# A decode block on one core: attention on two kv heads at a time with 32 KB descriptors and V as the moving operand, projections in row form

## The chip, the cores and the metric

One core of a Trainium2 chip runs the whole program. The metric is the device time of one execution in microseconds (us), as the median of the fast runs. PE is TensorE, DVE VectorE, ACT ScalarE, POOL GpSimd, SP SyncE, whose queue issues the loads. The kernel before takes 445.8 us.

## The reference, cut to what matters

One decode step of a block with adaptive layer norm, batch 8, all in bf16:

```python
mod = silu(c) @ w_mod                            # 8 x 6144: sa, ca, ga, sb, cb, gb
h = layernorm(x) * (1 + ca) + sa
q = h @ wq                                       # 32 heads of 128
o = softmax(q @ k_cache.T * 128**-0.5) @ v_cache # 8 x 4 kv heads, 8192 keys each, 8 q heads per kv head
x = x + ga * (o @ wo)
h = layernorm(x) * (1 + cb) + sb
x = x + gb * ((relu(h @ W_gate) * (h @ W_up)) @ W_down)
```

K and V are 134 MB, all weights 51 MB; every byte is used once. There are 32 pairs of batch and kv head ("heads" below); each has 2 MB of K and 2 MB of V.

## The kernel before

All large loads go through one ring in SBUF, `arena`, of nine 16 KB slots per partition. `load` only notes a transfer; `pump` is called after every operation and issues the next transfers, in order, on SP, as soon as the program has an operation that reads what lies in their place. The transfer itself then waits (by semaphore) until those reads are done. So the order of the loads is fixed, and a load that waits for its place holds back all the loads behind it.

```python
SLOT = 8192; NSLOT = 9                           # elements of bf16: 16 KB per partition
def pump():
    while stream:
        key, src, n = stream[0]
        lo = cursor[0] if cursor[0] + n <= NSLOT * SLOT else 0
        if P.unread("arena", lo, lo + n):
            return
        ...
        P.op("sp", lambda e: e.dma_start(dst, src), writes=[slot_r(lo, lo + n)], dma=True)
...
for n in range(N):                               # 32 heads: K, then V, 128 rows of 16 KB each
    load(("k", n), A_k_cache[n // G, n % G].rearrange("(p c) d -> p (c d)", p=128), SLOT)
    load(("v", n), A_v_cache[n // G, n % G].rearrange("(p c) d -> p (c d)", p=128), SLOT)
for i in range(4):
    load(("wo", i), wo_src[i], SLOT)             # "(q h d) n -> q d h n": rows of 2 KB
...
```

The attention turns K on DVE in quarters (`kt_part`), multiplies it with a padded q (`qk_part`, 512 columns moving), takes the maximum (`rowmax`, `spread`, `headmax`), the exponential on ACT (`expo`), turns it on DVE (`p_turn`), and multiplies with V (`pv`). In `pv`, V is the stationary operand, 64 weight loads of 128 x 128 for each head, and only 8 columns move:

```python
for cc in range(NC):                             # 64
    fns.append(lambda e, cc=cc: e.matmul(ps[:, 3, col:col + J], vv[:, cc, :], pv_[:, cc % 16, cc // 16, :], ...))
...
for n in range(N):
    kt_part(n + 1, 0)
    if n >= 1: p_turn(n - 1)
    kt_part(n + 1, 1)
    qk_part(n, 0); qk_part(n, 1); qk_part(n, 2); qk_part(n, 3)
    kt_part(n + 1, 2)
    if n >= 1: pv(n - 1)
    rowmax(n)
    kt_part(n + 1, 3)
    spread(n); headmax(n); expo(n); make_qpad(n + 2)
```

Gate and up are formed with weights stationary and 8 columns moving, too (448 matmuls); the output and down projections already stream weight rows of 256 columns through four column tiles of 32.

## Time and profile before

| | before |
|---|---|
| time, median | 445.8 us |
| span in the profile | 444.1 us |
| bytes moved, mean rate | 186 MB, 419 GB/s |
| DMA in the chain of waits | 83% |
| last weight landed (first engine / last engine) | 434.4 / 440.3 us |

From the profile's page of the kernel before: the span; the rows of forty slices (PEclk is the granted clock in tenths); the DMA queues; the chain; groups of instructions (count, busy us, mean ns, idle before them); two rows of DMA issues, with the us from issue to landing.

```profile
span 444.1 us, 7822 instructions
PE 290.9 (66%) x3514; PEld 165.4 (37%) x3514; DVE 217.7 (49%) x333; ACT 33.2 (7%) x78; POOL 30.8 (7%) x141
...
DMA  8999999999999999999999999999999999999993
GB/s 344 421 428 425 434 434 428 426 429 437 427 428 432 431 426 426 435 434 425 426 434 429 425 429 435 429 425 432 429 430 428 429 421 403 422 430 429 426 429 151
...
q8 instruction: 27, 0.44, 0.4%
...
DMA 83%; PE 8%; DVE 7%; issue 1%; ACT 0%; SPq 0%; POOL 0%; DVEq 0%; ACTq 0%; POOLq 0%
...
L411 DVE STREAM_TRANSPOSE kt<-arena 128x1024 uint32<-128x1024 uint32 x128 | 153.3, 1218 | 114.6 <-DMA arena<-in_A_k_cache_dram 114.6
L420 PE MATMUL ps<-kt,qpad 128*128 128x512 bf16 x512 | 161.5, 482 | 2.0 <-POOL qpad L400 2.0
...
L460 PE MATMUL ps<-pT,arena 128*128 128x8 bf16 x2048 | 56.0, 166 | 49.2 <-DVE pT L450 49.2
...
arena<-in_A_k_cache_dram SPq DMA_DIRECT2D x32, 2048.0 KB, 25.7
arena<-in_A_v_cache_dram SPq DMA_DIRECT2D x32, 2048.0 KB, 30.2
```

The GB/s row is flat near 430 from the second slice to the last but one; the one dip, 403, is the output weights. K is issued 25.7 us and V 30.2 us before it lands: with 4.9 us for a load of 2 MB, five to six loads are queued at any time.

Stretches of the attention of the kernel before (columns: stretch, its length, busy us of PE, of its weight loads, DVE, ACT and POOL with instruction counts, then the granted clock, the DMA share and GB/s):

```profile
180.00:240.00 60.00, 44.47 (x495) 24.18 (x496) 38.03 (x56) 4.67 (x12) 4.87 (x24) 0.80 1.01 430
240.00:300.00 60.00, 46.06 (x499) 23.84 (x498) 37.80 (x58) 4.67 (x12) 4.87 (x24) 0.81 1.01 430
300.00:360.00 60.00, 43.26 (x493) 23.38 (x492) 37.02 (x56) 5.44 (x14) 4.05 (x20) 0.82 1.01 429
```

The trace also records each DMA packet. Most packets of one size last the same time; these are medians of the kernels before and after, in ns:

```
bytes of a packet   2,048  4,096  8,192  14,336  16,384  24,576  28,672  32,768
took                   84    159    309     535     611     912   1,062   1,213
```

A packet starts 4 ns before the one ahead of it ends. The slope, (912 - 611) ns for 8,192 bytes, is 27.2 B/ns for an engine, and about 5 ns are left for each packet whatever its size.

### The profile page before, as it was taken

Reading aid. Unit: us, or ns where it says so; the run is one execution under the profiler, and the core shown is the slowest. Engines: PE = TensorE matmul, PEld = TensorE weight load, DVE = VectorE, ACT = ScalarE, POOL = GpSimd, SP = SyncE. Lnnn points to the kernel's source line nnn. Section 1 sums busy time; section 2 is a strip of 40 time slices with the busy share of each in tenths; the row PEclk is TensorE's granted clock in tenths of the full one; section 3 lists DMA queues with packets and bytes.
Section 4 is the critical chain, followed back from the end, with each engine's and each line's share of the span. In section 5 each row is a group of like instructions: output and inputs, shape, how many; then the busy total and the mean of one; then the engine's idle time right before and its main releaser. Section 6 shows DMA issues by size and latency. Waiting matters only on the chain.

```text
span 444.1 us, 7822 instructions
## 1 busy us (share of the span) xinstructions
PE 290.9 (66%) x3514; PEld 165.4 (37%) x3514; DVE 217.7 (49%) x333; ACT 33.2 (7%) x78; POOL 30.8 (7%) x141
## 2 busy tenths in 40 slices
PE   0235355677858676776877767786777787558753
PEld 0111022344434333443433334343333345348741
DVE  0503065666655566666555566665556664230000
ACT  0200010000001000000100000001000002000000
POOL 4000020100000001000000110000001000000000
PEclk9995576887788888879688888778888869655555
DMA  8999999999999999999999999999999999999993
GB/s 344 421 428 425 434 434 428 426 429 437 427 428 432 431 426 426 435 434 425 426 434 429 425 429 435 429 425 432 429 430 428 429 421 403 422 430 429 426 429 151
DMA packets 16770, 186.14 MB, mean 419 GB/s; under 512 B 1537, under 2 KB 1633, under 8 KB 5985
## 3 DMA queue, kind: packets, MB, share of 16 engines
q1 hardware_dynamic: 16704, 185.64, 98.5%
q8 instruction: 27, 0.44, 0.4%
q14 instruction: 7, 0.05, 0.0%
q10 hardware_dynamic: 32, 0.01, 0.0%
HBM read 185.63 MB, written 0.02 MB: 418 GB/s over the span
## 4 chain that ended last, share of the span: by engine, by line
DMA 83%; PE 8%; DVE 7%; issue 1%; ACT 0%; SPq 0%; POOL 0%; DVEq 0%; ACTq 0%; POOLq 0%
DMA arena<-in_A_k_cache_dram 62%; DMA arena<-in_B_W_down_dram 8%; DMA arena<-in_A_wq_dram 7%; DMA arena<-in_A_wo_dram 4%; PE ps L460 4%; DVE kt L411 3%; DMA c_r<-in_c_dram 2%; PE ps L528 1%; DVE pT L450 1%; PE ps L334 1%; PE ps L420 1%; PE ps L357 0%; DVE lu L281 0%; ACT L278 0%; DVE hT L286 0%
## 5 line engine op out<-in xcount | busy, mean ns | idle before, releaser
L411 DVE STREAM_TRANSPOSE kt<-arena 128x1024 uint32<-128x1024 uint32 x128 | 153.3, 1218 | 114.6 <-DMA arena<-in_A_k_cache_dram 114.6
L420 PE MATMUL ps<-kt,qpad 128*128 128x512 bf16 x512 | 161.5, 482 | 2.0 <-POOL qpad L400 2.0
L420 PEld LDWEIGHTS ps<-kt,qpad 128*128 128x128 bf16 x512 | 60.9, 119 | 91.8 <-issue 60.6
L460 PE MATMUL ps<-pT,arena 128*128 128x8 bf16 x2048 | 56.0, 166 | 49.2 <-DVE pT L450 49.2
L460 PEld LDWEIGHTS ps<-pT,arena 128*128 128x128 bf16 x2048 | 54.1, 96 | 63.6 <-issue 63.3
L400 POOL COPY qpad<-qR 32x32 bf16<-32x32 bf16 x128 | 26.0, 203 | 312.8 <-PE ps L420 256.0
L430 PE MATMUL ps<-identf,negm 128*128 128x128 f32 x64 | 20.2, 408 | 37.0 <-DVE negm L426 37.0
L444 ACT ACTIVATE prb<-ps,bias 128x512 bf16<-128x512 f32 x32 | 22.0, 687 | 283.9 <-DVE mjt L438 283.9
L528 PE MATMUL ps<-hT,arena 128*128 128x8 bf16 x448 | 24.8, 194 | 7.7 <-DMA arena<-in_B_W_up_dram 3.0
L528 PEld LDWEIGHTS ps<-hT,arena 128*128 128x128 bf16 x448 | 24.4, 153 | 8.1 <-DMA arena<-in_B_W_up_dram 3.2
L430 PEld LDWEIGHTS ps<-identf,negm 128*128 128x128 f32 x64 | 12.3, 240 | 40.3 <-DVE negm L426 40.3
L450 DVE STREAM_TRANSPOSE pT<-prb 128x512 bf16<-128x512 bf16 x32 | 21.5, 672 | 1.7 <-ACT prb L444 1.7
L426 DVE TENSOR_REDUCE negm<-ps 128x1 f32<-128x512 f32 x32 | 20.9, 653 | 1.0 <-PE ps L420 1.0
L535 DVE TENSOR_TENSOR hmT<-ps,grel 128x224 bf16<-128x224 f32 x1 | 0.4, 391 | 30.7 <-ACT grel L533 30.7
L357 PE MATMUL ps<-arena,hT 128*32 128x512 bf16 x64 | 7.6, 627 | 11.2 <-DMA arena<-in_A_wq_dram 8.4
L303 PE MATMUL ps<-st,sel 128*128 128x1 f32 x4 | 1.2, 362 | 19.3 <-DVE st L302 19.3
L334 PE MATMUL ps<-arena,hT 128*32 128x512 bf16 x96 | 9.0, 544 | 6.8 <-DMA arena<-in_w_mod_dram 6.8
L545 PE MATMUL ps<-arena,hmT 128*32 128x256 bf16 x112 | 7.1, 415 | 7.4 <-DMA arena<-in_B_W_down_dram 7.4
L509 PE MATMUL ps<-arena,oT 128*32 128x256 bf16 x128 | 6.4, 382 | 5.2 <-DMA arena<-in_A_wo_dram 2.6
L341 DVE COPY mod<-ps 128x512 f32<-128x512 f32 x2 | 1.3, 670 | 15.2 <-PE ps L334 15.2
L436 DVE TENSOR_REDUCE mj<-ps 128x8 f32<-128x128 f32 x32 | 8.1, 252 | 1.2 <-PE ps L430 1.2
L303 PEld LDWEIGHTS ps<-st,sel 128*128 128x128 f32 x4 | 1.0, 310 | 19.6 <-DVE st L302 19.6
(64 smaller groups left out, 66.0 us busy)
## 6 DMA issues: line engine op xcount, KB each, us to landing
arena<-in_A_k_cache_dram SPq DMA_DIRECT2D x32, 2048.0 KB, 25.7
arena<-in_A_v_cache_dram SPq DMA_DIRECT2D x32, 2048.0 KB, 30.2
arena<-in_w_mod_dram SPq DMA_DIRECT2D x4, 3072.0 KB, 18.2
arena<-in_A_wq_dram SPq DMA_DIRECT2D x4, 2048.0 KB, 35.0
arena<-in_A_wo_dram SPq DMA_DIRECT2D x4, 2048.0 KB, 19.1
arena<-in_B_W_gate_dram SPq DMA_DIRECT2D x4, 1792.0 KB, 24.2
arena<-in_B_W_up_dram SPq DMA_DIRECT2D x4, 1792.0 KB, 28.0
arena<-in_B_W_down_dram SPq DMA_DIRECT2D x3, 1792.0 KB, 33.8
```

The source lines that it names most:

```text
L334: fns.append(lambda e, w=w, pr=pr, j=j, kk=kk: e.matmul(ps[32 * j:32 * j + 32, pr, :], hT[:, kk, :], w[:, 2 * pr:2 * pr + 2, j, :], start= ...
L357: fns.append(lambda e, w=w, z=z, g=g, kk=kk: e.matmul(ps[32 * g:32 * g + 32, 3 + z, :], hT[:, kk, :], w[:, g, z, :], start=(kk == 0), stop ...
L400: P.op("pool", lambda e, n=n, Q=Q: e.tensor_copy(qpad[32 * Q:32 * Q + 32, n % NQ, :, 24 + 32 * Q:32 + 32 * Q], qR[32 * Q:32 * Q + 32, :, n ...
L411: P.op("dve", lambda e: e.transpose(ktb[:, to:to + QE].bitcast(dt.uint32), arena[:, lo:lo + QE].bitcast(dt.uint32)), reads=[slot_r(lo, lo ...
L420: fns.append(lambda e, t=t, r=r: e.matmul(ps[:, n % 2, :].rearrange("p (c k) -> p c k", k=32), qpad[:, n % NQ, t * 2 + r, 24 - 8 * i:152 - ...
L426: P.op("dve", lambda e: e.tensor_reduce(negm[:, n % 2:n % 2 + 1], ps[:, n % 2, :], AX.X, ALU.max, negate=True), reads=[bank(n % 2)], write ...
L430: P.op("pe", lambda e: e.matmul(ps[:, 2, 0:128], negm[:, n % 2:n % 2 + 1].to_broadcast([128, 128]), identf[:], start=True, stop=True), rea ...
L436: P.op("dve", lambda e: e.tensor_reduce(mj[:, z, :], ps[:, 2, 0:128].rearrange("p (m j) -> p j m", j=J), AX.X, ALU.min), reads=[bank(2)], ...
L444: P.op("act", lambda e: e.activation(prb[:, z, :], ps[:, z, :], ACT.Exp, bias=bias[:, z:z + 1], scale=scale, accum_out=lall[:, n:n + 1]), ...
L450: P.op("dve", lambda e: e.transpose(pT[:, z, :], prb[:, z, :]), reads=[R("prb", z, z + 1)], writes=[R("pT", z, z + 1)])
L460: fns.append(lambda e, cc=cc: e.matmul(ps[:, 3, col:col + J], vv[:, cc, :], pv_[:, cc % 16, cc // 16, :], start=(cc == 0), stop=(cc == NC ...
L528: fns.append(lambda e, w=w, f=f, kk=kk, off=off, first=first: e.matmul(ps[:, 0, off + f * B:off + (f + 1) * B], w[:, f // FR, f % FR, :], ...
```

## The change

The intent is fewer, longer DMA descriptors and fewer PE instructions: K and V come for two heads at once, 128 rows of 32 KB; V becomes the moving operand (512 columns) against the turned probabilities on two column tiles of 64; output, gate, up and down all stream weight rows, loaded in rows of up to 32 KB.

```diff
-        wo_src = A_wo.rearrange("(q h d) n -> q d h n", q=4, d=128)
+        wo_src = A_wo.rearrange("(p k) n -> p (k n)", k=KO)
...
-        for n in range(N):
-            load(("k", n), A_k_cache[n // G, n % G].rearrange("(p c) d -> p (c d)", p=128), SLOT)
-            load(("v", n), A_v_cache[n // G, n % G].rearrange("(p c) d -> p (c d)", p=128), SLOT)
-        for i in range(4):
-            load(("wo", i), wo_src[i], SLOT)
+        for m in range(M):                       # M = 16 pairs of heads
+            for nm, t in (("k", A_k_cache), ("v", A_v_cache)):
+                load((nm, m), t[m // 2, 2 * (m % 2):2 * (m % 2) + 2].rearrange("g (p c) d -> (g p) (c d)", p=64), 2 * SLOT)
+        wo_parts = [(0, 16), (16, 32)]
+        gu_parts = [(0, 4), (4, 8)]
+        wd_parts = [(0, 14), (14, 21), (21, 25), (25, 27), (27, 28)]
...
-        ktb = sb("kt", [128, 2 * SLOT], dt.bfloat16)
+        ktb = sb("kt", [128, 6 * 2048], dt.bfloat16)
...
+        def pv(m):                               # 32 matmuls of 512 columns for a pair
+            vv = arena[:, lo:lo + 2 * SLOT].rearrange("p (h i c d) -> p h c i d", h=2, i=4, d=Dh)
+            for t in range(32):
+                fns.append(lambda e, t=t: e.matmul(
+                    ps[64 * (t % 2):64 * (t % 2) + 64, 5, :].rearrange("p (i d) -> p i d", d=Dh),
+                    pT[:, z, t].rearrange("p g x -> p (g x)"), vv[:, t // 16, t % 16], ...,
+                    tile_position=(0, 64 * (t % 2))))
+        def fold(m):                             # four masked reads of PSUM on DVE, then one small matmul
...
+        for m in range(M):
+            for e8 in range(8):
+                kt_part(m, e8)
+                qk_part(m, e8)
+                if m >= 1:
+                    if e8 == 0:
+                        rowmax(m - 1, 1); spread(m - 1)
+                    elif e8 == 1:
+                        headmax(m - 1); expo(m - 1)
+                    elif e8 == 3:
+                        p_turn(m - 1)
+                    elif e8 == 4:
+                        pv(m - 1)
+                    elif e8 == 7:
+                        fold(m - 1)
+                if e8 == 5:
+                    rowmax(m, 0)
+            make_qpad(m + 2)
```

The ring is still nine slots of 16 KB, so four pair loads of 32 KB fit (K, V, K, V) and 16 KB are never used in the attention. The load of V for pair m+2 takes the place of V of pair m.

## The prediction

> **What bounds the kernel now.** HBM reading. The chain of waits is 83% DMA; the slices show the DMA engines full at 421 to 437 GB/s from the second slice on, except 403 where the output weights load. In the attention stage (60 to 360 us, table of stretches) PE is 0.7 to 0.75 busy, DVE 0.62. The Trainium skill ("DMA: Bandwidth & Descriptors", Specifications) puts the fabric ceiling at 435 GB/s. The trace agrees: its packet records last 611 ns for 16 KB, 912 for 24 KB, 84 for 2 KB: 27.2 B/ns per engine (435 GB/s on 16), plus about 5 ns per packet (a packet overlaps the next by 4 ns). So bandwidth can gain only about 1%.
>
> **What the change saves, per DMA engine (estimates from these durations).** KV: 512 packets of 607 ns become 256 of about 1,209: 1.3 us. Output weights: 256 of 80 ns become 16 of 1,209: 1.1 us. Gate, up: 0.1 us. 39 fewer DMAs, 6 ns for each semaphore packet: 0.2 us. Instruction fetches: 27 packets of 16 KB, which fit the 7,028 PE instructions, cost about 605 ns each, apparently on eight engines in turn (3.4 each). Moving V turns 2,048 PV matmuls into 512, and row form 448 gate/up matmuls into 128, so PE instructions halve and the engines that finish last gain about 1 us. All is on the critical path, because the DMA never pauses: 3.5 us together. The tail (bandwidth falls off from 434 to 440 us as engines finish apart, then 4 us of matmuls, two DVE ops, store) stays.
>
> **What it adds.** Per pair of heads (19.4 us of DMA) DVE rises from 13.6 us to about 16: two 64-partition turns of 1,024 columns (1.2 us each) and a fold of four PSUM reads (1.1 us), less one head-max. PE: QK as before (228 ns a matmul at full clock, 427 at half); PV as 16 concurrent pairs of 512 columns, 3.5 us at full clock, 6.8 at half (the wq matmuls show four column tiles sharing one 427 ns slot, weight loads hidden). Both fit. But buffers are fewer: four slots of 32 KB. I estimate that PV of a pair ends 14.4 us (warm) to 18.4 us (cold) after the next K lands; the V load needing this slot must be issued by about 18 us. Steady state should just hold. After attention the second gate load waits for the first output projection half: estimated issue 34.7 us after the last V, where the queue runs dry at 36.5 us, with 1 us of issue latency: I count 0.7 us of bubble.
>
> **Predicted:** 445.8 - 3.5 + 0.7 = 443.0 us, range 440.0 to 449.5 us. Chances: faster by over 2%: 0.02; within 2%: 0.88; slower: 0.10.
>
> **What would show it.** Right: packets near 1,213 ns for 32 KB, GB/s 430 to 433 in attention and output weights, 13 or 14 instruction fetches, DMA share near 1.0, last weight landing 2.5 to 3.5 us earlier. Wrong: dips in the GB/s row every 19.4 us (V issued late), a dip after the output weights (gate/up late), PE clock at half in most of the attention, the chain passing through PV and DVE instead of DMA.
>
> **What would make it wrong.** PV matmuls on two column tiles not overlapping (then PE needs over 19.4 us per pair); transposes on 64 partitions slower than estimated; longer rows striking HBM unfavourably; or, the other way, engines drifting apart less, which shortens the tail by up to 3 us.

## The result, and the profile after

The time after is 449.7 us (448.6 to 450.3, 4 runs) against 445.8 us: a ratio of 1.0084, 95% interval 1.0061 to 1.0107. Ratios here are the mean time of one kernel's fast runs over that of the other's of the same rounds, so they are not quite the ratio of the medians that are quoted. Executions over 1.5% slower than the fastest of the same kernel are left out of the means. The prediction was 443.0 us, range 440.0 to 449.5: the result lies outside, and the change lost time where the prediction had it gain.

The page of the changed kernel, the lines that answer to those of before:

```profile
span 447.5 us, 4025 instructions
PE 267.8 (60%) x1690; PEld 114.4 (26%) x1690; DVE 262.7 (59%) x371; ACT 28.8 (6%) x48; POOL 19.9 (4%) x77
...
DMA  8999999999999999999999999999899999999995
GB/s 348 415 435 425 447 434 429 428 431 436 429 431 404 435 451 422 425 414 428 425 432 387 428 423 390 425 425 438 363 442 377 439 425 420 440 418 396 419 427 212
...
q8 instruction: 13, 0.21, 0.2%
...
DMA 45%; PE 25%; DVE 24%; issue 5%; ACT 1%; SPq 0%; POOL 0%; DVEq 0%; ACTq 0%; POOLq 0%
...
L434 PE MATMUL ps<-kt,qpad 128*128 128x512 bf16 x512 | 148.1, 430 | 105.1 <-DVE kt L423 61.8
L423 DVE STREAM_TRANSPOSE kt<-arena 128x1024 uint32<-128x1024 uint32 x128 | 152.8, 1224 | 56.3 <-DMA arena<-in_A_k_cache_dram 55.9
...
L477 PE MATMUL ps<-arena,pT 128*64 128x512 bf16 x512 | 72.5, 447 | 4.5 <-DVE pT L468 4.5
...
arena<-in_A_k_cache_dram SPq DMA_DIRECT2D x16, 4096.0 KB, 24.3
arena<-in_A_v_cache_dram SPq DMA_DIRECT2D x16, 4096.0 KB, 14.8
```

Several things came as forecast: 13 instruction fetches instead of 27, packets of 1,213 ns for 32 KB, half the PE instructions. But the GB/s row has dips that were not there: 404, 387, 390, 363, 377 in the attention, the sign that the prediction had named for V loads issued too late, and 396 in the slice from 403 to 414 us, where the second gate load begins, its sign for late gate and up loads. And in the last line V is issued only 14.8 us before it lands, while one load now takes 9.7 us: at that moment little is left in the queue.

The same stretches as before, of the changed kernel:

```profile
180.00:240.00 60.00, 43.93 (x204) 17.98 (x204) 44.67 (x61) 3.61 (x6) 2.43 (x12) 0.83 0.99 419
240.00:300.00 60.00, 41.33 (x204) 17.24 (x204) 44.36 (x60) 3.61 (x6) 2.43 (x12) 0.89 0.99 418
300.00:360.00 60.00, 41.48 (x204) 17.32 (x204) 44.52 (x60) 3.61 (x6) 1.62 (x8) 0.89 0.97 410
```

PE is less busy than before at a higher clock, DVE is 74% busy: neither is full. The engine that lost is the DMA, from 430 to 410 to 419 GB/s, with its busy share nearly unchanged. The share hides the loss because packets at the start of a load that was issued too late are themselves recorded as longer (after the issue at 137.87 us also on engines that had not run dry: 1,792 ns for a packet that began right behind the one before it): after 60 us, 163 of the 4,234 packets of 32 KB last over 60 ns more than the usual 1,213 (up to 2,662 ns), in sum 4.4 us for each engine. Before, 25 of the 7,965 packets of 16 KB did (usual: 611 ns), in sum 0.7 us.

One turn of the loop in the changed kernel, from the timeline (start, length, engine and line; in brackets the idle time before): L423 is the turn of K, L477 is PV, L235 is the issue of V and then of the next K.

```profile
260.76 1.25 DVE L423 STREAM_TRANSPOSE kt<-arena 128x1024 uint32<-128x1024 uint32 x1 [4.66 <-DMA arena<-in_A_k_cache_dram]
...
269.66 2.37 DVE L423 STREAM_TRANSPOSE kt<-arena 128x1024 uint32<-128x1024 uint32 x2
...
271.93 5.33 PE L477 MATMUL ps<-arena,pT 128*64 128x512 bf16 x32
...
277.30 0.33 SPq L235 DMA_DIRECT2D arena<-in_A_v_cache_dram  x1
277.67 0.43 SPq L235 DMA_DIRECT2D arena<-in_A_k_cache_dram  x1
...
280.17 1.25 DVE L423 STREAM_TRANSPOSE kt<-arena 128x1024 uint32<-128x1024 uint32 x1 [1.35 <-DMA arena<-in_A_k_cache_dram]
```

K of pair 10 is there at 260.8 us. PV of pair 9 starts at 271.9, ends at 277.3, and only then are V of pair 11 and K of pair 12 issued. The next K, the last transfer in the queue, is complete at 280.1 us, but that is its slowest engine; its fastest was through at 277.6 us, 0.3 us after the issue. In another such place of the trace (V issued at 137.87 us) the first packet of the new load starts at 138.89 us: an issue takes 1.0 us to its first packet. So here the faster DMA engines stood still, for up to about 1 us.

The trace records each engine's signal that its part of a load has landed, so first and last engine can be told apart. "Landed" below is the us at which the first and the last of the 16 engines were through:

```
                       last V          output weights   last down weight
before             362.8 / 367.3      383.3 / 388.6      434.4 / 440.3
after              369.8 / 371.2      389.3 / 391.3      441.4 / 443.7
```

By the end of the attention the change is already 3.9 us behind (last engine; 7.0 us on the first one). The output weights then win back 1.2 us (21.3 us from the last V to their last landing, then 20.1), as forecast. The second gate load takes 9.7 us after the first up load where 8.5 is its packet time: another 1.2 us; it was issued at 404.9 us, 1.6 us before the first engine was through with all that was queued. Of the 1.2 us little is idle time: from 404 to 412 us the mean engine stood still for 0.2 us, and its packets took 0.8 us more than usual. From the last landing to the end of the span both kernels need 3.8 us.

### The profile page after: what moved, and what is told of

The parts are those of the page before. It is cut to its first block, busy times and chain, and to the rows that moved or that the text cites. A ratio compares the mean times of both kernels' runs of the same rounds, so it can differ in the third digit from the quotient of the medians.

```text
span 447.5 us, 4025 instructions
## 1 busy us (share of the span) xinstructions
PE 267.8 (60%) x1690; PEld 114.4 (26%) x1690; DVE 262.7 (59%) x371; ACT 28.8 (6%) x48; POOL 19.9 (4%) x77
## 4 chain that ended last, share of the span: by engine, by line
DMA 45%; PE 25%; DVE 24%; issue 5%; ACT 1%; SPq 0%; POOL 0%; DVEq 0%; ACTq 0%; POOLq 0%
DMA arena<-in_A_k_cache_dram 37%; DVE kt L423 12%; PE ps L477 11%; PE ps L434 8%; DVE pT L468 6%; DMA arena<-in_B_W_down_dram 6%; DMA c_r<-in_c_dram 2%; PE ps L562 1%; PE ps L347 1%; PE ps L583 1%; DVE negm L441 1%; DVE mj L452 1%; PE ps L447 1%; DVE mjt L455 0%; DVE kt L552 0%
## 5 line engine op out<-in xcount | busy, mean ns | idle before, releaser
L434 PE MATMUL ps<-kt,qpad 128*128 128x512 bf16 x512 | 148.1, 430 | 105.1 <-DVE kt L423 61.8
L423 DVE STREAM_TRANSPOSE kt<-arena 128x1024 uint32<-128x1024 uint32 x128 | 152.8, 1224 | 56.3 <-DMA arena<-in_A_k_cache_dram 55.9
L434 PEld LDWEIGHTS ps<-kt,qpad 128*128 128x128 bf16 x512 | 47.4, 105 | 189.1 <-DVE kt L423 89.1
L477 PE MATMUL ps<-arena,pT 128*64 128x512 bf16 x512 | 72.5, 447 | 4.5 <-DVE pT L468 4.5
L477 PEld LDWEIGHTS ps<-arena,pT 128*64 128x64 bf16 x512 | 32.6, 128 | 44.8 <-issue 28.6
L468 DVE STREAM_TRANSPOSE pT<-prb 64x1024 bf16<-64x1024 bf16 x32 | 39.0, 1220 | 1.8 <-ACT prb L461 1.3
L461 ACT ACTIVATE prb<-ps,bias 128x1024 bf16<-128x1024 f32 x16 | 17.8, 1113 | 289.2 <-DVE mjt L455 289.2
L416 POOL COPY qpad<-qR 32x32 bf16<-32x32 bf16 x64 | 13.0, 203 | 321.8 <-PE ps L434 269.2
L487 DVE SCALAR_TENSOR_TENSOR om<-ps,im,om 128x128 f32<-128x128 f32 x48 | 16.8, 351 | 1.7
L583 PE MATMUL ps<-arena,hT 128*32 128x448 bf16 x128 | 9.3, 457 | 10.1 <-DMA arena<-in_B_W_up_dram 6.8
L447 PE MATMUL ps<-identf,negm 128*128 128x128 f32 x32 | 8.4, 356 | 0.9 <-DVE negm L445 0.9
## 6 DMA issues: line engine op xcount, KB each, us to landing
arena<-in_A_v_cache_dram SPq DMA_DIRECT2D x16, 4096.0 KB, 14.8
```

The costliest lines, as they stand in the source:

```text
L416: P.op("pool", lambda e, n=2 * m + Q // 2, Q=Q: e.tensor_copy(qpad[32 * Q:32 * Q + 32, m % 2, :, 24 + 32 * Q:32 + 32 * Q], qR[32 * Q:32 * ...
L423: P.op("dve", lambda e: e.transpose(ktb[:, to:to + QE].bitcast(dt.uint32), arena[:, lo:lo + QE].bitcast(dt.uint32)), reads=[slot_r(lo, lo ...
L434: fns.append(lambda e, t=t, r=r: e.matmul(ps[:, b, :].rearrange("p (c k) -> p c k", k=32), qpad[:, m % 2, t * 2 + r, 24 - 8 * i:152 - 8 * ...
L447: P.op("pe", lambda e: e.matmul(ps[:, 4, 0:128], negm[:, 2:3].to_broadcast([128, 128]), identf[:], start=True, stop=True), reads=[R("negm" ...
L461: P.op("act", lambda e: e.activation(prb[:], ps[:, 2 * z:2 * z + 2, :].rearrange("p h n -> p (h n)"), ACT.Exp, bias=bias[:, z:z + 1], scal ...
L468: P.op("dve", lambda e, g=g: e.transpose(pT[64 * g:64 * g + 64, z, :, g, :], prb[64 * g:64 * g + 64, :]), reads=[R("prb"), R("pT", z, z + ...
```

## The experiments

Theory A: V is issued too late. With four slots its place comes free only when PV of the pair two back is done, 14 to 17 us after a K landed; by then the faster DMA engines are out of work, and each restart costs idle time and slow first packets. Rival B: a pair of heads is simply too much work for DVE and PE in its 19.4 us of DMA time (the chain of waits, with PE and DVE at 49%, looks like that). Rival C: transfers in 32 KB packets are slow by themselves. The eight kernels all gave correct results. The first four ran on one chip (the kernel before: median 446.5 us there), the other four on another (446.6 us); I compare by ratios to the kernel before of the same rounds.

### deep5: five slots instead of four

```diff
-    NSLOT = 9
+    NSLOT = 10
-        ktb = sb("kt", [128, 6 * 2048], dt.bfloat16)         # ring of 6 turned parts of K, then 4 (index % 6 -> % 4)
+        ktb = sb("kt", [128, 4 * 2048], dt.bfloat16)
-        pT = sb("pT", [128, 2, 32, 2, 32], dt.bfloat16)      # pT[z] with z = m % 2 -> z = 0
+        pT = sb("pT", [128, 1, 32, 2, 32], dt.bfloat16)
-        qrep = ktb[:, SLOT:SLOT + 4096]
+        qrep = ktb[:, 0:4096]
```

> The changed kernel with five 32 KB slots instead of four (room made by a kt ring of 4 parts instead of 6 and one pT buffer instead of two); packets, engine work and order of work are the same. Theory A (a V load can only be issued when PV of two pairs earlier is done, the DMA engines have run dry by then, and each restart costs idle time and slow first packets): the dry spells in attention vanish, last V lands at about 364 us instead of 371.2, time 441.5 to 444 us, faster than before by 0.5 to 1%. Theory B (DVE and PE have too much work per pair of heads for its 19.4 us of DMA): 449 to 450 us as now, because their work is the same. Theory C (32 KB packets themselves are slow at HBM or at the buffers): about 449 us, too.

Measured: 441.0 us (440.9 to 441.1), ratio 0.9878 (0.9861 to 0.9896), half a microsecond better than A's range; the last V landed at 365.1 us. The dips are gone, and in the stretches DVE and PE do the same work as in the changed kernel while the DMA is back at 432 to 434 GB/s. GB/s row and stretches of deep5:

```profile
GB/s 341 428 424 431 446 433 431 433 431 430 431 430 430 436 431 433 434 431 431 442 434 436 430 430 431 430 430 431 430 437 431 433 433 440 426 431 432 430 423 181
...
q8 instruction: 13, 0.21, 0.2%
```

```profile
180.00:240.00 60.00, 41.98 (x206) 17.32 (x207) 46.20 (x64) 3.61 (x6) 2.43 (x12) 0.88 1.00 432
240.00:300.00 60.00, 43.78 (x211) 18.16 (x210) 45.85 (x65) 3.61 (x6) 2.43 (x12) 0.87 1.00 433
300.00:360.00 60.00, 41.67 (x206) 17.36 (x205) 44.81 (x63) 3.92 (x7) 1.62 (x8) 0.87 1.01 434
```

This refutes B and C for the loss: the same engine work and the same packets, one slot more, take 2% less than the changed kernel (0.9878 / 1.0084 = 0.9796). The chain of waits would have misled: that of deep5 still has PV at 12% and the turns of K at 11%, much as in the changed kernel.

### pv3 and pv5: PV one part earlier, and one part later

```diff
 # pv3
                     elif e8 == 3:
                         p_turn(m - 1)
-                    elif e8 == 4:
                         pv(m - 1)
 # pv5
-                    elif e8 == 4:
+                    elif e8 == 5:
                         pv(m - 1)
```

(In pv3 `pv(m - 1)` follows `p_turn(m - 1)` directly, so PE does it ahead of QK part 4.)

> The changed kernel with PV of the pair before put one part earlier in PE's order (ahead of QK part 4 instead of behind it). Theory A: PV ends about 2 us earlier (12 to 14.5 us after a K lands instead of 14.2 to 16.5), so most dry spells go: 443 to 446 us. Theory B: same work, 449 to 450 us. Theory C: 449 to 450 us.

Measured: 441.0 us (440.4 to 441.2), ratio 0.9877 (0.9861 to 0.9892): the whole loss is gone with four slots, too, and the time is 2 us under the range that I expected. In this order PV also runs at full clock in every pair (3.6 us), so it ends 2.9 us earlier on average, not 2. From its page:

```profile
GB/s 348 424 422 432 444 433 432 430 434 430 432 430 436 433 432 430 431 432 428 436 433 429 436 438 436 430 430 429 430 436 433 433 430 429 432 432 430 433 418 205
...
q14 instruction: 5, 0.04, 0.0%
```

> The opposite dose: PV one part later (behind QK part 5). Theory A: V issued 1.5 to 2 us later, dry spells deeper, 452 to 460 us. Theory B: same work, 449 to 450 us, or a little more where the fold now waits. Theory C: 449 to 450 us.

Measured: 455.7 us (453.1 to 456.6), ratio 1.0198 (1.0168 to 1.0229), within A's range. The GB/s row of pv5 shows the dips of the changed kernel, deeper and more of them:

```profile
GB/s 348 425 422 432 445 425 435 432 422 437 409 434 431 428 369 419 429 386 432 385 444 399 434 386 440 425 359 438 416 451 320 434 419 373 413 438 411 439 409 214
```

For all four kernels I took from the traces, for the pairs 2 to 15, when PV ends and when V is issued, counted from the landing of the K of the pair in work, and how long the queue still lasts at that moment (until the next K, the last load issued, is through on the first and on the last engine). Means in us:

```
          PV end   V issued   queue left, first engine / last   from K to K   time
pv3        12.6      12.6             4.6 / 6.9                    19.5       441.0
after      15.5      15.5             2.1 / 4.4                    19.9       449.7
pv5        16.6      16.7             1.4 / 3.7                    20.3       455.7
deep5      15.6      -3.8            20.7 / 23.3                   19.5       441.0
```

The time follows what is left in the queue, not the moment of PV. In deep5 PV ends as late as in the changed kernel, and no less often at half clock, but V no longer waits for it; it is the next K load that takes the place of the old V, and when it is issued the first engine still has 10 to 12 us of work. The least a pair can take by its packets is 2 x (8 x 1.209 + 0.006) = 19.4 us. In the changed kernel PV ends 14.2 us after K at the earliest and 16.5 at the latest; in four of the fourteen pairs the first engine had 0.7 us or less left, under the 1.0 us that an issue takes. The late cases are those where PE ran a part of the time at half clock: PV then takes up to 5.3 us instead of 3.6.

What a late issue costs can be added up from the packets: time in which an engine has no packet, and time by which packets exceed the median of their size. From the landing of the first K to that of the last V, for the mean engine, in us:

```
                    before   pv3   after   pv5   deep5
no packet             0.0    0.0    3.5    7.1    0.0
longer packets        0.7    0.4    4.4    5.3    0.4
```

So the longer packets cost about as much as the standstill (0.4 us of them is there without any late issue). In the 8 us after each V issue of the changed kernel the two make 0.4 to 1.5 us at the seven issues with under 2 us left on the first engine, and at most 0.14 us at the seven with 2.8 us or more. Why those packets are longer is not shown.

### proj_only and attn_only: one half of the change each

proj_only is the kernel before with the loads and code of the new projections (from `wo_src` on); attn_only is the changed kernel with the old ones.

> The kernel before with only the projections changed (output, gate, up, down in row form with 28 to 32 KB descriptors), attention as before. All theories put the loss in attention, so: 444 to 445 us, that is 1 to 1.5 us under before, from 256 packets of 80 ns per engine that become 16 of 1,209 ns. If the second gate load comes late it loses a part of this; if it is above 446 us, the projections have a part in the loss.

Measured: 444.4 us (444.3 to 445.3), ratio 0.9959 (0.9944 to 0.9973). The projections alone gain 0.4%, about 1.8 us.

> The kernel before with only the attention changed (two heads at a time, 32 KB descriptors, V moving, four slots), the projections as before. Theory A (late V loads in the four-slot ring) puts the whole loss here: 450 to 452 us, about 1.2% over before, as the whole change is 0.84% over it and its projections alone are 0.4% under it.

Measured: 449.4 us (median of the five fast runs, 447.4 to 451.3; one slow run of 454.4 is left out), ratio 1.0066 (1.0042 to 1.0090). That is about half of the 1.2% that was forecast, but on the same side: the loss is in the attention. The sum of the halves, 0.66% - 0.41% = 0.25%, is under the 0.84% of the whole; the runs of attn_only scatter by 4 us, and the whole has the late second gate load (1.2 us), which neither half shows. I leave the rest of this difference open.

### deep5_16k: the descriptor size alone

```diff
-                load((nm, m), src, 2 * SLOT)
+                load((nm, m), src[:, 0:SLOT], SLOT)
+                load((nm, m, 1), src[:, SLOT:2 * SLOT], SLOT)
```

> The five-slot kernel with each K and V pair loaded in two DMAs of 16 KB descriptors; slots, releases and engine work as with 32 KB. My packet sum says 512 packets of 607 ns per engine for 256 of 1,209, and 64 DMAs for 32: 1.3 + 0.2 us more, 442 to 443 us against 441.0. If the descriptor size did more than that (theory D: long rows read better), 444 us or more; if nothing, 441 us.

Measured: 442.6 us (442.4 to 442.8), ratio 0.9914 (0.9902 to 0.9927). Against deep5 the ratio of ratios is 1.0036, that is 1.6 us; the packet sum had said 1.5. The two ran on different chips, and their intervals leave about 1 us either way. The size of the K and V descriptors is worth about this, and theory D is out.

### deep5_pv3: both remedies

> Five slots and the earlier PV together. Theory A: one remedy already ends the dry spells, so the second adds nothing: 440.5 to 441.3 us. If a rest of the loss were left, under 440 us.

Measured: 440.7 us (440.4 to 441.2), ratio 0.9869 (0.9855 to 0.9884), not distinguishable from either remedy alone, as A has it. It is the fastest median of all: 1.3% under the kernel before, 2.1% under the changed one (0.9869 / 1.0084).

### pv3_fetch: what an instruction fetch costs

Written first for deep5, where its scratch tile did not fit into SBUF, so it builds on pv3.

```diff
             make_qpad(m + 2)
+            P.op("pool", [lambda e, c=150 * m + i: e.memset(scr[0:32, c:c + 1], 0) for i in range(150)], writes=[R("scr", m, m + 1)])
```

> The kernel with earlier PV, and 2,250 tiny memsets on GpSimd added, which nothing waits for: about 9 more instruction fetches of 16 KB. If fetches cost their DMA engine about 0.6 us each, as the prediction took it, the mean engine loses 0.3 us and the late ones up to 0.7: 441.3 to 441.9 us against 441.0, and the last weight's first-to-last engine spread grows from 3.2 us. If they cost nothing, 441.0 us.

Measured: 451.9 us (451.6 to 452.6), ratio 1.0125 (1.0110 to 1.0139): by the medians 10.8 us more than pv3, far over what I had expected. (The loop runs 16 times, so there are 2,400 memsets.) Queue lines of pv3_fetch:

```profile
GB/s 353 407 437 424 456 420 434 441 429 420 436 444 423 430 438 434 430 427 444 411 422 420 414 425 396 430 391 436 399 417 402 409 437 372 423 434 392 438 411 143
...
q8 instruction: 13, 0.21, 0.2%
q14 instruction: 23, 0.19, 0.1%
```

Queue 14 has 18 packets more than in pv3 (5), of 8 KB each. The landings tell where they fell (us at which each of the 16 engines was through with K of pair 7):

```
pv3        196.6 196.8 197.1 197.3 197.3 197.4 197.6 197.7 197.8 198.0 198.1 198.1 198.1 198.1 198.2 198.2
pv3_fetch  196.6 196.7 196.9 197.5 197.5 197.5 197.7 197.8 197.9 198.0 198.0 198.1 198.2 198.2 198.2 202.3
```

Fifteen engines are where they were; one is 4 us late. I had assumed that the fetches spread over the engines; GpSimd's fall on one. Nearly all last 309 ns, and the data packet after each lasted 1,393 to 1,744 ns instead of 1,213, so a fetch costs its engine 0.5 to 0.9 us. Summed over the trace, this kernel's fetches on queue 14 cost 14.9 us and those of pv3 3.6: 11.3 us more, nearly all of it on the one engine that every load waits for, and the kernel is 10.8 us slower. With K landing later, V is issued later, and the other engines run dry in turn (V of pair 8 is issued with 1.1 us left on the first engine); so the dips in the row come back. That DVE or PE slowed down is not the reason: their busy time is 261.8 and 264.0 us, in pv3 261.6 and 260.9.

## Why the prediction was wrong

- **What bounds the kernel: right.** HBM reading at the rate of the DMA engines. The Trainium skill ("DMA: Bandwidth & Descriptors", Specifications) gives 435 GB/s as the fabric ceiling; the packet slope of 27.2 B/ns on 16 engines is 435 GB/s, too.
- **What the change saves: right in kind, too small.** With the dry spells gone (deep5) the first engine is through at 431.6 us instead of 434.4: 2.8 us, where the packet terms summed to 2.7. The last engine is through at 435.4 instead of 440.3: 4.9 us, where I had 3.5. The term that I mis-sized is "the engines that finish last gain about 1 us" from fewer instruction fetches: the spread between first and last fell by 2.1 us. I had put a fetch at 605 ns. The trace of before shows its packet of 16 KB at 879 to 1,082 ns (median 938), and the data packet behind it about 0.5 us longer than usual: 1.4 us in all for its engine, in deep5 and pv3 as well. With 27 fetches and then 13 on eight engines in turn, this makes 2.5 us for the late engines (an estimate from these numbers). That fetches delay single engines is shown by pv3_fetch; that the fewer PE fetches alone made these 2.1 us was not tested by itself.
- **PV on two column tiles: right.** 32 matmuls take 3.6 us at full clock (predicted 3.5). PV ended 14.2 to 16.5 us after K (predicted 14.4 to 18.4). DVE works about 14.8 us of a pair's 19.9 (44.5 of each 60 us), a little less than the predicted 16; before it was 12.3, not 13.6, so the rise of 2.5 us was close to the predicted 2.4.
- **"The V load needing this slot must be issued by about 18 us. Steady state should just hold": this step failed.** I counted the queue to the landing of the next K, 19.4 us, which is when the last engine is through. The engines drift apart by about 2.4 us (deep5: 196.7 to 199.0 us at K of pair 7), and an issue needs 1.0 us to its first packet, so for the fastest engine the limit is 19.4 - 2.4 - 1.0, about 16 us (an estimate from these numbers). The trace bears it out: V issues at up to 15.6 us after K cost at most 0.14 us, those at 15.9 and later 0.4 us or more. PV ends on average at 15.5 and in the cold pairs at 16.5. Both facts were in the trace of before: its engines are 4.6 us apart at the last V, and its first load, issued at 0.74 us, has its first packet at 1.77. I used the one for the tail and the other for the bubble, and left both out of the margin. Without this step the kernel is at 441.0 us (deep5, pv3); with it at 449.7: it cost 8.7 us by the medians (2%, or 9.2 us, by the ratios), the 1.2 us at the second gate load included, which both remedies end too.
- **The bubble at the second gate load: right in place, a little small.** Issued 33.7 us after the last V landed (predicted 34.7), cost 1.2 us (counted 0.7), mostly as longer packets, which I had not counted.
- **Signs named in advance.** "Dips in the GB/s row every 19.4 us (V issued late)" is what came, though at some pairs only: five dips for fourteen V loads. "A dip after the output weights (gate/up late)" came, too. A PE clock at half in most of the attention did not: it was 0.83 to 0.89 in the stretches. The chain passing through PV and DVE came, too, but it is no proof: it does so in deep5 as well.

So the change is sound, and its ring is one slot too short, or its PV one step too late, for loads twice as large. The Trainium skill has the general rule ("Perfetto Trace Analysis", Optimization Strategy): repeating gaps on the engine that should be saturated "can mean there isn't enough SBUF/PSUM for the next tile to be allocated (buffer count, tile sizes)". One slot more removed the gaps, and so did PV one part earlier without more memory.

## What to carry to other kernels

When descriptors or tiles are made larger in a ring of fixed size, recount the queue: for each load, take the moment when its slot comes free, and compare it with the moment when the fastest DMA engine runs out of work, not with the landing of the last transfer. Larger descriptors gained only 1.6 us in 445 here, and a ring that ran dry lost five times that; a consumer moved forward in the instruction order was as good a remedy as more memory. Look for dips in the GB/s row first; the chain of waits and the busy shares did not tell the bad version from the good one.

## What the Trainium skill lacked or had wrong

- "Runtime: NRT & Kernel Launch", Instruction fetch mechanics, says that crossing a 16 KiB block costs one DMA tail-bump, "mostly hidden", and that blocks hold 256 instructions. The blocks agree for PE (27 packets of 16 KB for 7,028 instructions, 13 for 3,380). The cost isn't hidden in a kernel bound by DMA: a fetch of PE takes its DMA engine 1.4 us and one of GpSimd 0.5 to 0.9 us, and 2,400 GpSimd instructions that nothing waits for made the kernel 10.8 us slower.
- The same section has blocks of 16 KiB for every engine; the 18 fetches that came with the GpSimd instructions are single packets of 8 KB, 3 us or more apart, and they delayed one DMA engine of the 16 (202.3 us against 198.2 or less). No page says on which DMA engines the fetches of an engine fall.
- "DMA: Bandwidth & Descriptors" tells to make a DMA at least 1 MiB, but no page says how much must be queued. Here 4 MB loads with 2.1 us left on the fastest engine at issue ran at 410 to 419 GB/s, with 4.6 us left or more at 430 and over.
- No page has how far the 16 engines drift apart over a long stream: 0.6 us at the first load, 4.6 us at the last V, 5.9 us at the end of the kernel before. A load lands with its slowest engine, and the queue runs dry with its fastest.
- No page tells that the first packets of a load that is issued too late take longer: up to 2.1 us instead of 1,213 ns after the issue at 137.87 us, and in the whole attention 4.4 us for the mean engine (pv3: 0.4), beside 3.5 us of standstill.
